# A planned Trainium2 kernel whose planner gets a transfer time for each kind of transfer

## The chip, the cores and the metric

The kernel runs on one core of a Trainium2 chip. The metric is the device time of one execution in microseconds (us); the time of a version is the median of several executions. TensorE (PE in the profile) multiplies matrices, VectorE (DVE), ScalarE (ACT) and GpSimd (POOL) work on elements, and SyncE (SP) issues most of the transfers (DMA) between memory and the core; GpSimd issues those that add into their target.

## The reference

The input `x` has 2048 rows of 512 numbers. The block normalises it and feeds it to two branches, whose product is added to `x`.

```python
x = A_x
xn = _layernorm(x, axis=-1)
s = _A_ref(xn, A_wqkv, A_wo)                   # linear attention, 32 heads of 16
g = _silu(_B_ref(xn, B_w1, B_w2, B_w3, B_w4))  # mixer with an MLP, 512 -> 1376 -> 512
return x + s * g

# A: phi = lambda t: where(t > 0, t + 1, exp(t)) + 1e-6, on q and k
kv = einsum("bhsd,bhse->bhde", pk, v);  z = einsum("bhsd->bhd", pk)
o = einsum("bhqd,bhde->bhqe", pq, kv) / (einsum("bhqd,bhd->bhq", pq, z)[..., None] + 1e-6)
s = o @ wo
# B: spatial shift of four groups of channels by +1, -1, +2, -2 rows, then the MLP
h = gelu(layernorm(x) @ w1);  x1 = x + shifted(h) @ w2
B = x1 + gelu(layernorm(x1) @ w3) @ w4
```

## The kernel before

Everything is float32. A product is made of three matmuls on parts rounded to a shorter type (`hi` and `lo`, written by `rounded` and `products`), and larger products use a seven-product scheme (`seven`). The 2048 rows are 16 tiles of 128 rows, in four blocks `b` of 512.

In the first part, to about 220 us, `x` and its transpose `xt` are loaded; keys and queries are formed and their Gram matrix is summed over all tiles in four accumulators (`gram`, tiles `g`); `w1` is centred (its column means are subtracted: `Weights.center` sums the four chunks of `w1` into `w1t` by gathers of GpSimd, the matmul `w1m` spreads the mean, and DVE subtracts it from the pieces `w_s`); `mix1` gives the tiles `h`, whose first matmuls need the centred pieces `w_0h`, `w_0l` and so on; `mix2` gives `x1`, which is normalised, turned by 32 x 32 blocks and written out (`Turned.put`). In the second part, for each block, `turn_y` fetches the turned tiles back in four pieces each (`y_0t`, `y_1t`), `up_pair` and `down` are the MLP, `turn_q` and `attend_pair` the attention (tiles `so`, accumulators `pbs` and others), and `gate` joins both and stores the result.

No engine's order is written by hand. The program first lists some 5,070 operations (`Plan.add`), each with its engine, the tiles that it reads and writes, and a duration; each is numbered in the order in which it is listed. `Plan.emit` then simulates the five engines and two queues and always emits the operation that can start first; among those that can start at about the same time it takes the one with the earliest due time. A matmul's due time is its place in the listed order; that of another operation is worked back from what needs it (`deadlines`, `backward`). The table `SOONER` then moves the due times of single operations by a quarter of a microsecond per unit (`nudged`). The emitted order is each engine's order on the chip; waits between engines are then semaphores.

What the simulation holds of a transfer is three lines in `emit`: one shared resource `dma`, on which transfers follow each other at 3.43 us per MB from SP and 4.59 from GpSimd, a fixed time to the landing, and a shortest time from issue to landing. An operation that needs a transfer is held back by up to `SAFE`, 2 us, behind the planned landing, if its due time leaves room for that. At most eight transfers of a queue are under way in the plan.

Of the kernel before, what the change touches and what calls it, by code (L numbers as in the profile page):

```python
# [11 lines left out]
ALU = mybir.AluOpType  # L12
AX = mybir.AxisListType

P = 128
# [11 lines left out]
class Tile:  # L27
# [16 lines left out]
    @property  # L44
    def all(self):
        return self[:, :]
# [5 lines left out]
class View:  # L52
# [3 lines left out]
    def get(self):  # L56
        return self.fn(self.tile.ap)
# [24 lines left out]

class Op:
    __slots__ = ("eng", "busy", "lat", "emit", "pre", "post", "tiles", "opens", "two", "table", "patience", "soon", "loads",
                 "nom", "due", "ready", "at", "end", "mb", "order")


class Plan:
# [9 lines left out]
    def add(self, eng, busy, lat, reads, writes, emit, two=False, table=None, mb=0.0):  # L98
        op = Op()
        op.eng, op.busy, op.lat, op.emit, op.two, op.table, op.mb = eng, busy, lat, emit, two, table, mb  # L100
        op.pre, op.post, op.tiles, op.opens = {}, [], {}, False
        op.order = len(self.ops)
        op.patience, op.soon = self.patience, False
        op.loads = any(isinstance(v, View) and v.tile.tag != "dram" for v in writes)
        for views, write in ((reads, False), (writes, True)):
            for v in views:
                if not isinstance(v, View):
                    continue
                t = v.tile
                op.tiles[t] = True  # L110
                op.opens |= not t.log and t.tag in self.counts
                for spans, other, wrote in t.log:
                    if other is op or not (write or wrote):
                        continue
                    if any(a < d and c < b for a, b in v.spans for c, d in spans):
                        flow = wrote and not (eng == "PE" and other.eng == "PE" and write)
                        op.pre[other] = op.pre.get(other, False) or flow
        for views, write in ((reads, False), (writes, True)):
            for v in views:
                if isinstance(v, View):  # L120
                    if write:
                        v.tile.log = [e for e in v.tile.log
                                      if not all(any(a <= c and d <= b for a, b in v.spans) for c, d in e[0])
                                      or e[1] is op]
                    v.tile.log.append((v.spans, op, write))
        for o in op.pre:
            o.post.append(op)
        for t in op.tiles:
            t.left += 1
        if eng == "PE":  # L130
            self.last_pe = op.order
        self.ops.append(op)
        return op
# [68 lines left out]
                 lambda: self.nc.vector.scalar_tensor_tensor(out.get(), a.get(), get(s), b.get(), op0=op0, op1=op1),  # L202
                 True, isinstance(s, View))

    def load(self, out, src, eng="SP"):
        mb = out.n * P * 4 / 1e6
        e = self.nc.scalar if eng == "ACT" else self.nc.sync
        self.add(eng, .42, 0, [], [out], lambda: e.dma_start(out.get(), src), mb=mb)

    def store(self, dst, src):  # L210
        mb = src.n * P * 4 / 1e6
        if isinstance(dst, View):
            return self.add("SP", .42, 0, [src], [dst], lambda: self.nc.sync.dma_start(dst.get(), src.get()), mb=mb)
        else:
            self.add("SP", .42, 0, [src], [], lambda: self.nc.sync.dma_start(dst, src.get()), mb=mb)

    def fetch(self, out, src):

        mb = out.n * P * 4 / 1e6
        self.add("SP", .42, 0, [src], [out], lambda: self.nc.sync.dma_start(out.get(), src.get()), mb=mb)  # L220

    def gather(self, out, src, share=1.0):

        mb = out.n * P * 4 / 1e6 * share
        return self.add("POOL", .8, 0, [src, out], [out],
                 lambda: self.nc.gpsimd.dma_start(out.get(), get(src), accum_op=ALU.add), mb=mb)  # L226

    GAP = .06  # L230
    PATIENCE = 2.5
# [38 lines left out]
    def emit(self, first, lead, reserve, window, ahead, table=()):  # L270
# [13 lines left out]
        port, dma = 0.0, 0.8  # L284
# [6 lines left out]
        while left:  # L291
# [5 lines left out]
            for e, cands in avail.items():  # L297
                picks = []
                low = INF
                for op in cands:  # L300
                    s = max(free[e], op.ready)
                    if op.mb:
                        s = max(s, under[e == "POOL"][0] + self.GAP)
                    if op.two and s < port:
                        s = port
                    if e == "POOL" and not op.mb and not op.two:
                        s = next((b + .02 for a, b in lock if a <= s < b), s)
                    if op.table is not None and op.table != table:
                        s = max(s, free[e] + 1.28)
                    ok = True  # L310
                    fresh = [t for t in op.tiles if t.ap is None]
                    for t in fresh:
# [7 lines left out]
                        s = max(s, q[need - 1][0] + self.GAP)  # L320
# [4 lines left out]
                        elif t.tag in lead:  # L325
# [3 lines left out]
                            s = max(s, op.due + slip - n - t.early)  # L329
# [12 lines left out]
                s, op = min(((s, op) for q, s, op in picks if q <= low + slack), key=lambda x: (x[1].due, x[1].order))  # L342
# [4 lines left out]
            s, op = best  # L347
            e = op.eng
# [12 lines left out]
            op.end = s + op.lat * k  # L361
            if op.mb:
                soft = e == "POOL"
                late = min(.92, 1.03 * max(0.0, dma - s))
                dma = max(dma, s + (.97 if soft else .06)) + op.mb * (4.59 if soft else 3.43)
                op.end = max(dma + (1.89 if soft else 1.29) + late, s + (4.08 if soft else 2.08 if op.loads else 2.2))
                under[soft].pop(0)
                under[soft].append(op.end)
            if op.two:
# [29 lines left out]
def linear_attn_gated_by_mixer(  # L399
# [22 lines left out]
    BT = QT * P  # L422
    FB = -(-F // P)
    W = 4
# [21 lines left out]
    pl = Plan(nc, pools, counts, ("acc", "mm"))  # L446

    def piece(name, dt=F32):
        return pl.new("p", name, dt, PIECE)[:, :512]
# [5 lines left out]
    def memory(name, width=512, rows=P):  # L455
        return pl.new("dram", name, F32, width, rows)
# [29 lines left out]
    def rounded(hi, lo, full, src=None):  # L486

        pl.act(hi, src or full, AF.Copy)
        split(lo, full, hi)
# [15 lines left out]
    arow, mrow = memory("arow", S + 2 * EDGE, 1), memory("mrow", S, 1)  # L505
# [136 lines left out]
    def join_a(b):  # L642

        t = ABC[b] = pl.new("ab", f"abc{b}", F32, BT + W)
        a = EDGE + b * BT - 2
        pl.fetch(t.all, arow[:, a:a + BT + W].via(lambda ap: ap.to_broadcast([P, BT + W])))

# [31 lines left out]
    def make_u(b):  # L679

        m = piece(f"um{b}")
        pl.fetch(m, mrow[:, b * BT:(b + 1) * BT].via(lambda ap: ap.to_broadcast([P, BT])))
        for c in range(NC):
            pl.tt(XT[b, c], XT[b, c], m, ALU.subtract)
            rounded(*(t[:, 2:2 + BT] for t in UT[b][c]), XT[b, c])
        q = {(t, k): [XT[b, 2 * k + c].cols(t * TH, (t + 1) * TH) for c in range(2)]
             for t in range(2) for k in range(2)}
        U[b] = {n: [both([v[:, 2:2 + BT] for v in UT[b][2 * k + c]], t * TH, (t + 1) * TH) for c in range(2)]
                for n, t, k in (("a11", 0, 0), ("a12", 0, 1), ("a22", 1, 1))}
        s = [piece(f"us{b}_{k}") for k in range(4)]  # L690
        parts = [[v.cols(c * TH, (c + 1) * TH) for c in range(2)] for v in s]
        for n, u, v, op in ((0, q[1, 0], q[1, 1], ALU.add), (1, parts[0], q[0, 0], ALU.subtract),
                            (2, q[0, 0], q[1, 0], ALU.subtract), (3, q[0, 1], parts[1], ALU.subtract)):
            for c in range(2):
                pl.tt(parts[n][c], u[c], v[c], op, eng=SUMS)
            hl = rounds(f"us{b}_{n}")
            rounded(*hl, s[n])
            U[b][f"s{n + 1}"] = [both(hl, c * TH, (c + 1) * TH) for c in range(2)]
# [42 lines left out]
    class Turned:  # L741
# [15 lines left out]
        def take(self):  # L757
            self.w = w = 512 * self.n
            t = self.t = pl.new("w" if self.n == 2 else "p", f"{self.name}t", F32, 1024 if self.n == 2 else PIECE)
            nb = P // RB  # L760
            for n in range(nb):
                src = self.d.cut([(0, 512)], w // nb, lambda ap, n=n: ap.rearrange(
                    "(a k) (b f) -> b k a f", k=RB, b=nb)[n])
                dst = t.cut([(n * w // nb, (n + 1) * w // nb)], w // nb, lambda ap, n=n: ap[
                    n * RB:(n + 1) * RB, :w].rearrange("k (a f) -> k a f", f=P))
                pl.fetch(dst, src)

        def part(self, c0, c1):

# [627 lines left out]
    b = NQ - 1  # L1397
# [6 lines left out]
    for base, s in ((0, 1), (DH - 1, -1)):  # L1404
        v = bmask.all.via(lambda ap: ap.rearrange("p (h d) -> p h d", d=DH))
        pool(.5, [v], v, lambda v=v, base=base, s=s: g.affine_select(
            out=v.get(), in_=v.get(), compare_op=ALU.is_ge, fill=0.0, base=base,
# [33 lines left out]
    for b in range(NQ):  # L1441
# [46 lines left out]
        else:  # L1488
# [3 lines left out]
            t = piece(f"xi{i}", F32R)  # L1492
# [13 lines left out]
                gate(b * QT + QT - 1, a, o, D // 2, late=True, by_dma=False, whole=o > 0)  # L1506

    SOONER = (
# [3 lines left out]
    )  # L1512
    pl.emit(first=6.0, lead={"p": 14.0, "w": 14.0, "ab": 10.0}, reserve={"p": 20, "w": 1, "ab": 0}, window=12.0,
            ahead=6.0, table=SOONER)
# [37 lines left out]
```

## Time and profile before

| | us |
|---|---|
| median of three executions | 514.07 |
| the three executions | 514.64, 514.07, 512.39 |
| the profiled execution | 512.43 |
| its span, from the first to the last instruction | 510.7 |
| TensorE busy in the span | 502.9 |
| VectorE, ScalarE, GpSimd busy | 426.3, 348.9, 91.2 |

The granted TensorE clock was 1.00 in the whole span. A row of a list of waits names the engine and the tile that waited, after the arrow what it waited for, and then the total time, the number of times and the longest one. A row of the chain of waits gives start, duration and what the time was spent on. "L" and a number is a line of the kernel; most operations are recorded by a few helpers, so one goes by the names of the tiles.

### The profile page before, as it was taken

The numbers are of one execution on the slowest core, as the hardware profiler recorded it, in microseconds if no ns is written. First come the engines' busy times: TensorE is split into PE (matmuls) and PEld (weight loads), VectorE is DVE, ScalarE is ACT, GpSimd is POOL, SyncE is SP. The second block draws the span as 40 slices with busy tenths as digits, with TensorE's granted clock in tenths as the row PEclk, the third lists the DMA queues.
The fourth block names the chain that finished last, engine by engine and source line by source line (L and its number), as shares of the span: only waits on it lengthen the run. The fifth ranks groups of instructions, "written<-read, shape, count | busy, mean of one in ns | idle before, by whom it ended". The sixth has DMA issues, their size and how long they took to land.

```text
span 510.7 us, 8948 instructions
## 1 busy us (share of the span) xinstructions
PE 502.9 (98%) x2972; PEld 437.9 (86%) x2972; DVE 426.3 (83%) x885; ACT 348.9 (68%) x703; POOL 91.2 (18%) x145
## 2 busy tenths in 40 slices
PE   9998999999999999999999999999999999999995
PEld 7777777898888788889989898999898998999985
DVE  6999999999699986999999978956779656898645
ACT  5899699676697785866876668655488453765621
POOL 1258411663134122021000020000020000200000
PEclk9999999999999999999999999999999999999999
DMA  8889947189994799799767758475495595758604
GB/s 270 310 185 226 303 151 167 41 201 295 278 284 92 239 292 270 199 271 313 247 204 205 224 137 280 160 215 154 164 230 183 181 222 166 182 185 265 195 14 111
DMA packets 76619, 106.17 MB, mean 208 GB/s; under 512 B 8224, under 2 KB 31292, under 8 KB 76572
## 3 DMA queue, kind: packets, MB, share of 16 engines
q1 hardware_dynamic: 68940, 91.70, 56.4%
q0 software_dynamic: 7632, 13.90, 16.1%
q8 instruction: 23, 0.38, 0.3%
q14 instruction: 24, 0.20, 0.1%
HBM read 67.41 MB, written 29.77 MB: 190 GB/s over the span
## 4 chain that ended last, share of the span: by engine, by line
PE 86%; DVE 5%; ACT 5%; DMA 2%; issue 1%; SPq 1%; DVEq 0%; ACTq 0%
PE acc L148 23%; PE pb L148 11%; PE h L148 8%; PE g L148 7%; PE pbk L148 6%; PE pe L148 5%; PE pbm L148 4%; PE pbs L148 4%; PE pek L148 3%; PE pa L148 3%; PE pem L148 2%; PE a L148 2%; PE pes L148 2%; DMA y_1t<-y_1d 2%; PE pak L148 1%
## 5 line engine op out<-in xcount | busy, mean ns | idle before, releaser
L226 POOL DMA_DIRECT2D th<-in_x x14 | 12.2, 939 | 248.0 <-DVE so L192 64.8
L170 ACT ACTIVATE th<-xo 128x512 f32<-128x512 f32 (+1 forms) x16 | 9.8, 620 | 26.8 <-DVE xo L192 26.6
L192 DVE TENSOR_TENSOR xo<-acc,xo 128x512 f32<-128x512 f32 (+1 forms) x16 | 10.5, 671 | 16.9 <-PE acc L148 16.8
L170 ACT ACT_TABLE_LOAD x18 | 23.1, 1283 | 1.1 <-PEq L1543 0.8
L170 ACT ACTIVATE gf<-gf 128x512 f32<-128x512 f32 (+1 forms) x40 | 20.6, 525 | 0.8
L226 POOL DMA_DIRECT2D o<-x x16 | 14.0, 873 | 40.1 <-DVE o L192 15.5
L226 POOL DMA_DIRECT2D zacc<-kr x16 | 13.9, 867 | 40.6 <-DMA zacc<-kr 22.2
L170 ACT ACTIVATE p<-pb 128x256 f32<-128x256 f32 x20 | 7.6, 382 | 14.2 <-PE pb L148 14.0
L604 POOL TENSOR_TENSOR rs<-w,nhalf 128x4 f32<-128x4 f32 (+2 forms) x10 | 10.1, 1012 | 35.5 <-DVE w L197 32.6
L170 ACT ACTIVATE p<-pe 128x256 f32<-128x256 f32 x20 | 7.7, 385 | 11.9 <-PE pe L148 11.9
L170 ACT ACTIVATE ht<-ht 128x512 f32<-128x512 f32 x16 | 9.7, 623 | 8.9 <-DVE ht L192 8.9
L192 DVE TENSOR_TENSOR gf<-pa,p 128x256 f32<-128x256 f32 x20 | 8.4, 420 | 7.8 <-PE pa L148 7.5
L170 ACT ACTIVATE x<-x,nm,rs 128x512 f32<-128x512 f32 x16 | 12.9, 807 | 2.5 <-DVE nm L202 2.5
L598 DVE BATCH_NORM_STATS2 st<-o 128x6 f32<-128x512 f32 x16 | 10.9, 686 | 3.5 <-DMA o<-x 3.4
L192 DVE TENSOR_TENSOR gf<-u,pe 128x256 f32<-128x256 f32 x20 | 8.2, 410 | 6.5 <-PE pe L148 6.5
L202 DVE SCALAR_TENSOR_TENSOR kr<-kt,kr 128x512 f32<-128x512 f32 x16 | 10.9, 688 | 1.8 <-ACT kt L170 1.7
L170 ACT ACTIVATE y<-o,nm,rs 128x512 f32<-128x512 f32 x16 | 11.9, 807 | 0.5 <-DVE nm L202 0.5
L192 DVE TENSOR_TENSOR ht<-h,abc 128x512 f32<-128x512 f32 x16 | 10.9, 683 | 0.8 <-PE h L148 0.6
L202 DVE SCALAR_TENSOR_TENSOR pq<-pq,qr 128x512 f32<-128x512 f32 x12 | 8.1, 683 | 4.1 <-ACT pq L170 4.0
L170 ACT ACTIVATE u<-pb 128x256 f32<-128x256 f32 x20 | 7.7, 383 | 5.5 <-PE pb L148 5.5
L202 DVE SCALAR_TENSOR_TENSOR th<-th,so 128x512 f32<-128x512 f32 (+1 forms) x17 | 10.9, 653 | 0.5
L202 DVE SCALAR_TENSOR_TENSOR pq<-pq,rd 128x512 f32<-128x512 f32 x16 | 10.9, 688 | 0.2
(1679 smaller groups left out, 2235.5 us busy)
## 6 DMA issues: line engine op xcount, KB each, us to landing
w_s<-in_w SPq DMA_DIRECT2D x28, 256.0 KB, 4.3
x<-in_x SPq DMA_DIRECT2D x16, 256.0 KB, 5.3
zacc<-kr POOLq DMA_DIRECT2D x16, 256.0 KB, 5.9
o<-x POOLq DMA_DIRECT2D x16, 256.0 KB, 4.9
x1d<-o SPq DMA_DIRECT2D x16, 256.0 KB, 4.2
xo<-x1d SPq DMA_DIRECT2D x16, 256.0 KB, 5.0
xt<-in_xt SPq DMA_DIRECT2D x15, 256.0 KB, 5.0
out<-th SPq DMA_DIRECT2D x15, 256.0 KB, 3.4
```

The costliest lines, as they stand in the source:

```text
L148: lambda: nc.tensor.matmul(out.get(), lhs.get(), rhs.get(), start=start, stop=stop, skip_group_check=more))
L170: nc.scalar.activation(out.get(), src.get(), func, scale=get(scale), **kw)
L192: self.vec(eng, out, [a, b], lambda: self.e(eng).tensor_tensor(out.get(), a.get(), b.get(), op=op), True)
L202: lambda: self.nc.vector.scalar_tensor_tensor(out.get(), a.get(), get(s), b.get(), op0=op0, op1=op1),
L226: lambda: self.nc.gpsimd.dma_start(out.get(), get(src), accum_op=ALU.add), mb=mb)
L598: pl.add("DVE", .62, .69, [xv], [st], lambda: nc.vector.bn_stats(st.get(), xv.get()))
L604: lambda: g.tensor_tensor(out.get(), src.get(), nh.get(), op=ALU.pow))
```

## The change

The list of operations stays the same. Each transfer gets a kind, with its own time per MB: load (from an input), fetch (from a scratch tensor), row (one row spread over all partitions), turn (the pieces of a turned tile), store and gather. The constants around it change too, in a new method `landing`; the planned issue time of GpSimd's transfers goes from 0.8 to 0.6 us; and the table `SOONER` is another one.

```diff
-    def load(self, out, src, eng="SP"):
-        mb = out.n * P * 4 / 1e6
-        e = self.nc.scalar if eng == "ACT" else self.nc.sync
-        self.add(eng, .42, 0, [], [out], lambda: e.dma_start(out.get(), src), mb=mb)
+    def move(self, eng, out, src, kind, mb, reads, writes, emit):
+        op = self.add(eng, .42 if eng == "SP" else .6, 0, reads, writes, emit, mb=mb)
+        op.rate = self.RATE[kind]
+        return op
+
+    def load(self, out, src):
+        return self.move("SP", out, src, "load", out.n * P * 4 / 1e6, [], [out],
+                         lambda: self.nc.sync.dma_start(out.get(), src))
...
     def gather(self, out, src, share=1.0):
-
-        mb = out.n * P * 4 / 1e6 * share
-        return self.add("POOL", .8, 0, [src, out], [out],
-                 lambda: self.nc.gpsimd.dma_start(out.get(), get(src), accum_op=ALU.add), mb=mb)
-
-
+        return self.move("POOL", out, src, "gather", out.n * P * 4 / 1e6 * share, [src, out], [out],
+                         lambda: self.nc.gpsimd.dma_start(out.get(), get(src), accum_op=ALU.add))
+
+    RATE = {"load": 2.92, "fetch": 3.5, "row": 4.18, "turn": 5.7, "store": 2.44, "gather": 5.79}
+
+    def landing(self, op, s, dma):
+
+        soft = op.eng == "POOL"
+        dma = max(dma, s + (.33 if soft else 0)) + op.mb * op.rate
+        late = min(1.11, .68 * max(0.0, dma - s))
+        return dma, max(dma + (1.36 if soft else 1.25) + late, s + (3.77 if soft else 1.97 if op.loads else 1.68))
...
                 soft = e == "POOL"
-                late = min(.92, 1.03 * max(0.0, dma - s))
-                dma = max(dma, s + (.97 if soft else .06)) + op.mb * (4.59 if soft else 3.43)
-                op.end = max(dma + (1.89 if soft else 1.29) + late, s + (4.08 if soft else 2.08 if op.loads else 2.2))
+                dma, op.end = self.landing(op, s, dma)
...
     SOONER = (
-        23, 127, 94, 16, 119, -16, 128, 16, 132, 2, 183, 4, 291, 8, 322, 16, 333, 72, 394, -4, 412, -32, 418, -64,
-        423, -101, 424, -64, 426, -17, 427, 44, 429, 8, 483, 16, 612, 16, 749, 32, 1599, -8, 2185, 32, 2781, -8,
-        3582, 16, 3853, 32, 4261, 8, 4798, -32, 4917, 8, 4980, -8, 4994, -32, 4996, 8,
+        9, 64, 23, 17, 94, 32, 119, -8, 128, 16, 132, 2, 183, 4, 269, -8, 291, 8, 333, 72, 336, 16, 357, 2,
+        394, -4, 415, -124, 448, 8, 455, 32, 612, 16, 1599, -8, 1728, -8, 1976, 4, 2287, 64, 2350, 4, 2393, 16,
+        2431, 32, 3017, 32, 3582, 16, 3853, 32, 3932, -8, 4086, 8, 4662, 16, 4798, -32, 4917, 8,
     )
```

The calls in `join_a` and `make_u` pass the kind "row", and those in `Turned.take` the kind "turn". Some of the numbered operations: 9 is the store of a zero edge of `arow`, 23 the first load of `xt`, 412, 415 and 418 are matmuls of the Gram matrix of tile 3, 423 and 424 split `w1t` into `w1mh` and `w1ml`, 426 is the matmul `w1m` on the second, 427 and 429 subtract it from pieces of `w1`, and 455 is the copy `kq_0h`.

More of the change, by code (lines that the diff above doesn't have):

```diff
@@ L84 @@
     __slots__ = ("eng", "busy", "lat", "emit", "pre", "post", "tiles", "opens", "two", "table", "patience", "soon", "loads",
-                 "nom", "due", "ready", "at", "end", "mb", "order")
+                 "nom", "due", "ready", "at", "end", "mb", "order", "rate")
 class Plan:
@@ L102, in add @@
         op.order = len(self.ops)
-        op.patience, op.soon = self.patience, False
+        op.patience, op.soon, op.rate = self.patience, False, 0.0
         op.loads = any(isinstance(v, View) and v.tile.tag != "dram" for v in writes)
@@ L203, in stt @@
                  True, isinstance(s, View))
-    def load(self, out, src, eng="SP"):
-        mb = out.n * P * 4 / 1e6
-        e = self.nc.scalar if eng == "ACT" else self.nc.sync
-        self.add(eng, .42, 0, [], [out], lambda: e.dma_start(out.get(), src), mb=mb)
-    def store(self, dst, src):
[L211 to L215, printed above, removed]
@@ L217, in fetch @@
-    def fetch(self, out, src):
-        mb = out.n * P * 4 / 1e6
-        self.add("SP", .42, 0, [src], [out], lambda: self.nc.sync.dma_start(out.get(), src.get()), mb=mb)
-    def gather(self, out, src, share=1.0):
-        mb = out.n * P * 4 / 1e6 * share
-        return self.add("POOL", .8, 0, [src, out], [out],
-                 lambda: self.nc.gpsimd.dma_start(out.get(), get(src), accum_op=ALU.add), mb=mb)
+    def move(self, eng, out, src, kind, mb, reads, writes, emit):
+        op = self.add(eng, .42 if eng == "SP" else .6, 0, reads, writes, emit, mb=mb)
+        op.rate = self.RATE[kind]
+        return op
@@ new lines, in load, with fetch @@
+    def load(self, out, src):
+        return self.move("SP", out, src, "load", out.n * P * 4 / 1e6, [], [out],
+                         lambda: self.nc.sync.dma_start(out.get(), src))
+    def store(self, dst, src):
+        return self.move("SP", dst, src, "store", src.n * P * 4 / 1e6, [src], [dst] if isinstance(dst, View) else [],
+                         lambda: self.nc.sync.dma_start(get(dst), src.get()))
+    def fetch(self, out, src, kind="fetch"):
+        return self.move("SP", out, src, kind, out.n * P * 4 / 1e6, [src], [out],
+                         lambda: self.nc.sync.dma_start(out.get(), src.get()))
@@ L645, in join_a @@
         a = EDGE + b * BT - 2
-        pl.fetch(t.all, arow[:, a:a + BT + W].via(lambda ap: ap.to_broadcast([P, BT + W])))
+        pl.fetch(t.all, arow[:, a:a + BT + W].via(lambda ap: ap.to_broadcast([P, BT + W])), "row")
     UT = {}
@@ L681, in make_u @@
         m = piece(f"um{b}")
-        pl.fetch(m, mrow[:, b * BT:(b + 1) * BT].via(lambda ap: ap.to_broadcast([P, BT])))
+        pl.fetch(m, mrow[:, b * BT:(b + 1) * BT].via(lambda ap: ap.to_broadcast([P, BT])), "row")
         for c in range(NC):
@@ L765, in take @@
                     n * RB:(n + 1) * RB, :w].rearrange("k (a f) -> k a f", f=P))
-                pl.fetch(dst, src)
+                pl.fetch(dst, src, "turn")
         def part(self, c0, c1):
```

## The prediction

> **What bounds the kernel now.** I read the page first, then a table of windows, then TensorE's own waits, and then the chain of waits around each of them.
>
> ```profile
> span 510.7 us, 8948 instructions
> PE 502.9 (98%) x2972; PEld 437.9 (86%) x2972; DVE 426.3 (83%) x885; ACT 348.9 (68%) x703; POOL 91.2 (18%) x145
> PE 86%; DVE 5%; ACT 5%; DMA 2%; issue 1%; SPq 1%; DVEq 0%; ACTq 0%
> ```
>
> TensorE is busy for 502.9 of 510.7 us, and the chain that ended last runs on it for 86% of the span. The change leaves the 2972 matmuls as they are, so an order can only win back what lies between them: 510.7 - 502.9 = 7.8 us. The table of windows says where that is (first column: the stretch; then its length and the busy time of each engine, PE first).
>
> ```profile
> core 0: us, PE busy (x) PEld busy (x) DVE busy (x) ACT busy (x) POOL busy (x), PEclk, DMA share, GB/s
> 0.00:14.00 14.00, 12.96 (x50) 9.98 (x51) 9.42 (x17) 8.15 (x15) 2.24 (x14) 1.00 0.83 282
> 14.00:42.80 28.80, 27.51 (x120) 21.25 (x118) 27.44 (x69) 27.01 (x57) 14.55 (x24) 1.00 0.82 222
> 42.80:64.00 21.20, 21.13 (x89) 16.46 (x90) 21.09 (x39) 16.00 (x28) 13.14 (x26) 1.00 1.01 294
> 64.00:220.00 156.00, 156.00 (x832) 132.33 (x831) 141.59 (x309) 120.35 (x226) 45.99 (x65) 1.00 0.76 209
> 220.00:420.00 200.00, 200.00 (x1321) 180.47 (x1320) 164.52 (x334) 132.54 (x283) 10.09 (x11) 1.00 0.73 212
> 420.00:426.00 6.00, 5.69 (x42) 5.02 (x42) 4.80 (x10) 3.54 (x10) 0.00 (x0) 1.00 0.63 145
> 426.00:505.60 79.60, 79.60 (x530) 72.38 (x528) 56.16 (x110) 40.93 (x89) 5.22 (x6) 1.00 0.57 164
> 505.60:510.70 5.10, 0.00 (x1) 0.00 (x0) 1.30 (x4) 0.38 (x1) 0.00 (x0) 0.96 0.35 126
> ```
>
> Of the 7.8 us, 1.04 lie ahead of the first matmul, 1.29 just ahead of 42.8 us, 0.07 in the next 21 us, 0.31 between 420 and 426 us, and 5.10 behind the last matmul. From 64 to 420 us and from 426 us to the end TensorE has no idle time at all. The ends of matmuls are modelled, so a little may be hidden in a busy stretch, but not much. TensorE's list of waits names the inner two:
>
> ```profile
> PE h L148 <- ACT w_0h L170: 1.3, 1, 1.3
> PE warm L148 <- POOL ones L511: 1.0, 1, 1.0
> PE pbs L148 <- ACT u2s L170: 0.3, 1, 0.3
> ```
>
> The 1.0 us ahead of the warm-up matmuls waits for a memset and belongs to no transfer. The last 5.10 us are the last gate and its store, one operation behind another. So what can be had in the profiled execution is 1.29 + 0.07 + 0.31 = 1.7 us.
>
> **The wait at 42.8 us.** It ends on an ACT copy, `w_0h`, the first piece of the centred `w1`. The timeline of ACT and DVE, and GpSimd's at 31 us, show what stood ahead of it (start, duration, engine, line, operation):
>
> ```profile
> 36.34 1.32 ACT L170 ACTIVATE qe<-qt,ns 128x512 f32<-128x512 f32 x2
> 37.56 1.14 ACT L170 ACTIVATE qe<-qe 128x512 f32<-128x512 f32 x2
> 38.60 0.61 ACT L170 ACTIVATE w1mh<-w1t 128x512 fp32r<-128x512 f32 x1
> 39.13 1.32 ACT L170 ACTIVATE qr<-qt,rs 128x512 f32<-128x512 f32 x2
> 40.35 0.71 ACT L170 ACTIVATE qe<-qt,ns 128x512 f32<-128x512 f32 x1
> 40.97 0.61 ACT L170 ACTIVATE u_1h<-xt 128x512 fp32r<-128x512 f32 x1
> 42.01 0.61 ACT L170 ACTIVATE w_0h<-w_s 128x512 fp32r<-128x512 f32 x1
> ...
> 41.14 1.88 DVE L202 SCALAR_TENSOR_TENSOR w_s<-w1m,w_s 128x512 f32<-128x512 f32 x3
> ...
> 30.95 0.90 POOL L226 DMA_DIRECT2D w1t<-in_w  x1
> 31.55 0.95 POOL L707 CAST u_0h<-hal 128x2 fp32r<-128x2 f32 x1
> ```
>
> `w1mh` needs the sum `w1t`, whose last gather is issued at 30.95 us; the list of DMA issues below gives these gathers a median of 5.1 us to landing, so the sum is there at about 36.1 us. ACT takes it up at 38.60 us, 2.5 us later, behind four copies of queries (`qe`, 36.34 to 38.70). The stall is thus a matter of order on ACT and DVE, not of a late transfer: in 14 to 42.8 us ACT is busy for 27.01 and DVE for 27.44 of 28.80 us. Putting `w1mh` ahead of the `qe` pairs would bring the chain forward by up to 2.5 us, and the matmul that waits needs 1.29.
>
> **The wait at 423 us.** The chain of waits shows a transfer behind this one:
>
> ```profile
> 414.64 7.74 DMA y_1t<-y_1d
> ...
> 422.48 0.63 ACT yb123h L170
> 423.11 0.28 ACT u2s L170
> ...
> 423.44 0.97 PE pbs L148 x6
> ```
>
> `yb123h` sits at the head of ACT's in-order queue until the fourth piece of `y_1t` has landed, 7.74 us after its issue, and `u2s`, which releases the accumulator `pbs`, stands behind it. The old model gave each such 128 KB piece 0.131 x 3.43 = 0.45 us, the new one 0.131 x 5.7 = 0.75, so four of them together land 1.2 us later in the new plan; a planner that believes this puts `u2s` ahead of `yb123h`, or the fetch earlier.
>
> **The change, part by part.** *The rates.* No instruction comes or goes, so nothing in it has a cost on the chip; what changes is what the planner believes, and with it each engine's order. One 256 KB transfer is 0.262 MB: on SP it was 0.90 us, and becomes 0.77 (load), 0.92 (fetch), 1.10 (row) or 0.64 (store); a gather goes from 1.20 to 1.52. Medians to landing at 256 KB (`y_1t` 128 KB) are these:
>
> ```profile
> x<-in_x SPq DMA_DIRECT2D x16, 256.0 KB, 5.3
> o<-x POOLq DMA_DIRECT2D x16, 256.0 KB, 4.9
> xo<-x1d SPq DMA_DIRECT2D x16, 256.0 KB, 5.0
> out<-th SPq DMA_DIRECT2D x15, 256.0 KB, 3.4
> xs<-in_x SPq DMA_DIRECT2D x8, 256.0 KB, 7.7
> y_1t<-y_1d SPq DMA_DIRECT2D x16, 128.0 KB, 5.4
> w1t<-in_w POOLq DMA_DIRECT2D x3, 256.0 KB, 5.1
> ```
>
> They bear out the kinds at the ends: a store lands in 3.4 us, and `y_1t` takes 5.4 for half the bytes. They don't show a gather (`o`, 4.9 us) as dearer than a fetch (`xo`, 5.0), and they do not bear out a cheap load: `x` needs 5.3 us and `xs` 7.7, but both hold the time in the queue. I take the direction as right and the size of the load as doubtful.
>
> [...]
>
> *GpSimd's issue*, 0.8 to 0.6 us in the plan: the rows at 30.95 and 31.55 start 0.60 us apart, so it comes nearer to the chip. Nothing on the chain waits for it; cost 0, at most one issue's 0.2 us either way.
>
> *The hand-set due times* (SOONER; numbers are operations in program order, a unit is 0.25 us). Those on `w1`'s centring go (423, 424, 426, 427, 429), and with them two of the Gram matmuls put off (412, 418); another Gram matmul (415, the third chunk of tile 3) is put off by 31 us, which leaves TensorE other work for just the place where it waits 1.29 us; `kq_0h` (455) gets due 8 us earlier and joins ACT's queue there. The first load of `xt` (23) is hurried by 4.25 us in place of 31.75, and a store of the zero edge of `arow` (9) by 16 us. This store goes to SP's queue among the first loads and costs one issue, 0.4 us at most for what is queued behind. Bounds for the opening, then: between all of the 1.29 us won, and a wait that is longer than now by one transfer. The longest row of the same kind, `xs` at 7.7, is 2.4 us over `x` at 5.3; so -1.3 to +2.4. I take -1.3, nearest to the rows above, for these show 2.5 us of ACT work that could stand behind.
>
> *The turn's rate*, at 423 us: -0.3 us, bounds -0.3 and +0.7; the upper one is where ACT's queue blocks for as long as the chain rows from 422.48 to 423.44 show, 0.96 us, in place of 0.31.
>
> *The executions.* The profiled one took 512.43 us, 1.73 more than its span of 510.7; the three timed ones took 514.64, 514.07 and 512.39. The median is 1.64 us above the profiled time. Two executions sit at 512.4 and two at 514 or above, with the same program, so some wait comes and goes; the place where the profile shows a transfer eating its whole margin is the turn before 423 us, and there are others like it after each block of 512 rows. A plan that prices turns, fetches and gathers higher leaves more room there. I put 1.2 of the 1.64 us down as won; bounds 0 and 1.64. This is the weakest term.
>
> The sum: in the profiled execution 512.43 - 1.3 - 0.3 = 510.8; against the median 514.07 - 1.3 - 0.3 - 1.2 = 511.3 us, 0.54% faster. About 0.5%, or 2.57 us, is what a measurement of this kernel can tell from no change.
>
> **The rivals.** *No room (same).* The two inner waits go, or are exchanged for others as small, but the coming and going of 1.64 us has nothing to do with the plan: 514.07 - 1.6 = 512.5 us. It covers too the case that the new table gives much the same order: outside 3 us of waits TensorE is seamless, and 356 us of the middle have nothing to win. For it: the windows. Against it: the spread of the executions at an unchanged program.
>
> *Late landings in the opening (slower).* Between 14 and 64 us ACT and DVE have next to no idle time (DVE 21.09 of 21.20 us in the second stretch), and each engine keeps its order. The new plan holds loads to be 15% cheaper than the old one (2.92 against 3.43), so it may put an operation at the head of ACT or DVE whose load isn't there yet, and all that is queued behind (the `w1` pieces, `u` pieces, keys) is late by as much; nothing later makes it up, since TensorE has no idle time to give. One such landing costs 7.7 - 5.3 = 2.4 us if it falls on a chain that TensorE waits for. Two of them, one ahead of `w_0h` with the 1.29 us still there, and one in the 20 us behind it, give 514.07 + 4.8 = 518.9 us; one gives 516.5. It decides from where loads land over 2 us later than planned, for the planner keeps 2 us (SAFE) behind every transfer when the due time allows. For it: load rows that differ by 2.4 us at one size. Against it: the rows of PE's waits hold no transfer at all now, so the margins hold.
>
> **How the numbers follow.** The forecast gets 0.45, no room 0.30, late landings 0.25. Faster by over 0.5% needs under 511.5 us, which only the forecast gives; its own range runs from 510.8, with all three terms full, less about 1.2 that seamless stretches may hide (an estimate: the six `pbs` matmuls at 423.44 take 0.97 us, and a few such stretches would have to shrink), to 511.5. Late landings pass 516.6 with a little over one. The range, 509.6 to 518.0, leaves out about 0.05 below and 0.12 above, the dearer half of late landings. Chances: faster 0.45, same 0.30, slower 0.25.
>
> **What would show it.** Right: TensorE's waits without `w_0h`, or with under 0.5 us there; ACT taking `w1mh` up within about 1 us of the landing of `w1t`; no wait near 423 us; TensorE's busy time again near 502.9 us and a span near 509; executions closer together. Wrong: a wait at `h` of over 1.3 us, a new wait on a DMA in the first 64 us, or a seamless stretch of the middle that has gaps. If the span falls by 1.6 us and the median doesn't move as far, the term for the executions is what failed.

## The result, and the profile after

| | before | changed |
|---|---|---|
| median of 22 executions, us | 512.41 | 514.36 |
| lowest to highest | 511.33 to 514.98 | 512.70 to 516.52 |
| profiled execution, span | 512.43, 510.7 | 513.31, 511.6 |

The changed kernel is slower: the ratio of its time to that before is 1.0028, 95% interval 1.0015 to 1.0040. (The ratio of the two means, 514.44 and 513.01, is the same; that of the medians is 1.0038.) The change is smaller than the 0.5% that the prediction named, but clear of no change, and it goes the other way. The median before is also 1.66 us below that of the three executions on which the prediction stood; with 22 executions it lies where the profiled one lay.

The page of the changed kernel, its span, two of its engines and the chain:

```profile
span 511.6 us, 8924 instructions
PE 503.6 (98%) x2972; PEld 438.5 (86%) x2972; DVE 425.3 (83%) x885; ACT 348.2 (68%) x703; POOL 93.8 (18%) x145
PE 95%; DMA 2%; DVE 2%; ACT 0%; issue 0%; SPq 0%
```

```profile
0.00:14.00 14.00, 12.53 (x47) 9.49 (x47) 8.69 (x16) 8.28 (x14) 2.23 (x14) 1.00 0.84 273
14.00:42.80 28.80, 28.16 (x120) 21.53 (x119) 26.07 (x67) 25.96 (x53) 15.21 (x27) 1.00 0.82 213
42.80:64.00 21.20, 19.99 (x87) 15.77 (x86) 21.19 (x39) 16.47 (x30) 10.06 (x24) 1.00 1.05 299
64.00:220.00 156.00, 156.00 (x822) 131.88 (x821) 141.17 (x308) 120.44 (x226) 50.13 (x64) 1.00 0.77 208
220.00:420.00 200.00, 200.00 (x1322) 180.76 (x1321) 164.43 (x335) 130.72 (x280) 10.97 (x12) 1.00 0.74 213
420.00:426.00 6.00, 6.00 (x48) 5.68 (x46) 4.32 (x10) 5.32 (x13) 0.00 (x0) 1.00 0.76 189
426.00:506.00 80.00, 80.00 (x531) 72.64 (x531) 57.32 (x111) 40.63 (x89) 5.16 (x6) 1.00 0.57 162
```

In the windows (columns as before) the middle is as seamless as it was, the 0.31 us at 423 us are gone, and all that TensorE idles between its first and its last matmul lies in the first 64 us. There DVE is busy for 26.07 us between 14 and 42.8 us, where it was busy for 27.44. TensorE's waits:

```profile
PE h L148 <- ACT w_0h L170: 1.2, 1, 1.2
PE warm L148 <- POOL ones L514: 1.0, 1, 1.0
PE g L148 <- DVE k3l L202: 0.5, 1, 0.5
PE k L148 <- DMA wk_s<-in_wqkv: 0.4, 1, 0.4
```

The wait for `w_0h` is still there, and two are new: one ahead of the Gram matmuls of tile 3 (on the keys `k3l`), and one ahead of the first matmul `k` (on the first weights `wk_s`). Followed back from `h`, the chain of waits of the changed kernel between 29 and 45 us reads in extract (start, duration, what):

```profile
29.63 3.46 DMA mrow<-cr
...
33.11 4.04 DMA um<-mrow
...
37.17 0.69 DVE xt L192
37.86 0.60 DVE kr L202
...
40.27 0.60 DVE k3l L202
...
42.13 0.60 DVE w1ml L192
42.73 0.61 DVE xt L192
43.33 0.69 DVE w_s L202
...
44.05 0.64 ACT w_0h L170
...
44.73 1.42 PE h L148 x5
```

Two transfers in a row, a store of one row of means (`mrow`) and its fetch onto all partitions (`um`), now hold DVE in this execution, and all that is queued on DVE behind the first subtraction of `um`: the keys of tile 3, `w1ml`, the centring `w_s`. DVE's timeline has the wait in its brackets, and the kernel before has the same subtraction behind the other work, with no wait:

```profile
37.17 0.69 DVE L192 TENSOR_TENSOR xt<-xt,um 128x512 f32<-128x512 f32 x1 [1.34 <-DMA um<-mrow]
37.77 0.69 DVE L202 SCALAR_TENSOR_TENSOR kr<-kt,kr 128x512 f32<-128x512 f32 x1
```

```profile
36.59 0.69 DVE L202 SCALAR_TENSOR_TENSOR k3l<-kr,k3h 128x512 fp32r<-128x512 f32 x1
...
39.00 0.68 DVE L192 TENSOR_TENSOR xt<-xt,um 128x512 f32<-128x512 f32 x1
```

The kernel's own planner says why. These are its planned times beside the traced ones (the planner's clock is taken to start 0.68 us after that of the traces):

```
                      um: planned issue, landing    planned    traced     DVE's first subtraction of um
before                34.96, 40.10                  5.14 us    4.02 us    planned at 40.65
changed               32.69, 35.78                  3.09 us    4.04 us    planned at 35.85
end of TensorE's work, planned: before 504.03, changed 502.74; on the chip, less 0.68: 504.92 and 506.25
```

The old model overrated this transfer by 1.1 us, the new one underrates it by 0.95. By plan the changed order was 1.3 us better; on the chip it is 1.3 us worse. The same turn shows at the first `h`: planned at 44.37 before and 43.44 in the changed kernel, it came at 42.09 and 44.05 on the planner's clock.

### The profile page after: what moved, and what is told of

Its sections match the earlier page's. It is cut to its first block, busy times and chain, and to the rows that moved or that the text cites. A ratio compares the mean times of both kernels' runs of the same rounds, so it can differ in the third digit from the quotient of the medians.

```text
span 511.6 us, 8924 instructions
## 1 busy us (share of the span) xinstructions
PE 503.6 (98%) x2972; PEld 438.5 (86%) x2972; DVE 425.3 (83%) x885; ACT 348.2 (68%) x703; POOL 93.8 (18%) x145
## 4 chain that ended last, share of the span: by engine, by line
PE 95%; DMA 2%; DVE 2%; ACT 0%; issue 0%; SPq 0%
PE acc L148 23%; PE pb L148 11%; PE h L148 9%; PE g L148 7%; PE pbk L148 7%; PE pe L148 6%; PE pbs L148 5%; PE pbm L148 5%; PE pek L148 3%; PE pa L148 3%; PE k L148 2%; PE pem L148 2%; PE pes L148 2%; PE a L148 2%; PE pak L148 2%; PE q L148 2%
## 5 line engine op out<-in xcount | busy, mean ns | idle before, releaser
L607 POOL TENSOR_TENSOR au<-pu,nhalf 128x4 f32<-128x4 f32 x4 | 8.2, 2058 | 19.9 <-DVE pu L197 14.6
L170 ACT ACTIVATE so<-pbs 128x256 f32<-128x256 f32 x8 | 3.1, 385 | 12.7 <-PE pbs L148 12.7
L192 DVE TENSOR_TENSOR so<-pas,p1s 128x256 f32<-128x256 f32 x8 | 3.4, 420 | 9.7 <-PE pas L148 4.7
```

The costliest lines, as they stand in the source:

```text
L170: nc.scalar.activation(out.get(), src.get(), func, scale=get(scale), **kw)
L192: self.vec(eng, out, [a, b], lambda: self.e(eng).tensor_tensor(out.get(), a.get(), b.get(), op=op), True)
L607: lambda: g.tensor_tensor(out.get(), src.get(), nh.get(), op=ALU.pow))
```

## The experiments

The theory (A): the loss is made in the opening, because the changed plan counts on landings that come later; and it is the cheap price of the load that does it, not the table (A1). A narrower form (E): it is the one wait on `um`. Rivals: the long second part (B), the table (A2), the fixed times (C), the ratio of the kinds (D), and for the last runs something else that the price of the row moves (F).

**Which part of the program.** Two kernels have both models and change from one to the other at 64 us of planned time; the table's entries to operation 749 go with the first model.

```diff
-                dma, op.end = self.landing(op, s, dma)
+                new = s >= 64.0
+                dma, op.end = (self.landing if new else self.before_landing)(op, s, dma)
+                if soft and not new:
+                    free[e] = s + .8
```

`before_opening` has this text, `after_opening` has `s < 64.0`. On every engine their planned orders are those of the kernels that they are named for up to 95 us at least.

> The order of the kernel before up to 64 us, planned on from there with the changed rates and the later part of the changed table. Theory A (the loss is made in the opening, where the changed plan counts on transfers landing sooner than they do): like before, 512.4 us or less, within 0.1% of it. Theory B (the loss is made in the long second part, by collisions of transfers that come and go): like after, about 514 us, 0.25% over before.

> The order of the changed kernel up to 64 us, planned on from there with the rates before and the later part of the table before. Theory A: like after, about 514 us, 0.25% over before, with the DVE wait on um of about 1.3 us at 36 us. Theory B: like before, 512.4 us, within 0.1%.

Measured: `before_opening` 1.0001 (0.9986 to 1.0015), though with a median of 513.25 us, 0.7 over that of before. So the changed rates and table cost at most 0.15% from 64 us on, and B falls. `after_opening` came out at 1.0067 (1.0042 to 1.0091) in six executions, slower than either theory had it. Its windows show 1.06 us that TensorE idles between 64 and 420 us, where both parents are seamless; the rest of its loss is open.

```profile
64.00:220.00 156.00, 155.65 (x821) 131.08 (x820) 140.47 (x307) 120.03 (x225) 50.88 (x65) 1.00 0.76 207
220.00:420.00 200.00, 199.29 (x1310) 178.95 (x1310) 161.31 (x327) 127.78 (x276) 10.71 (x12) 1.00 0.71 207
```

Theory A expected a wait of DVE on `um` of 1.3 us here, and its profiled execution has none. The order is that of the changed kernel, but SP could issue the fetch 2.50 us after the store of `mrow`, in place of 3.48, and DVE took up the first subtraction of `um` without a wait:

```profile
29.39 0.27 SPq L216 DMA_DIRECT2D mrow<-cr  x1
31.89 0.34 SPq L220 DMA_DIRECT2D um<-mrow  x1
...
35.51 0.69 DVE L192 TENSOR_TENSOR xt<-xt,um 128x512 f32<-128x512 f32 x1
```

From the first `k` to the first `h` it needed 37.77 us, 1.72 less than the changed kernel's profiled execution. So the wait costs about that much in this pair, and the order alone doesn't bring it about: it takes a late landing too. How many of the changed kernel's executions have it, one profile can't tell.

**Rates or table.** `new_rates_old_table` is the changed kernel with the old `SOONER`, `old_rates_new_table` the kernel before with the new one; nothing else is edited.

> The changed rates with the table of due times before. Theory A1 (the rates themselves are too hopeful in the opening): about 514 us, 0.25% over before, PE's end over 2.5 us behind the plan's 503.96. Theory A2 (only the changed table puts the um subtraction too early): within 0.1% of before. A table that was set for other rates may add up to 1 us under both.

> The rates before with the changed table. Theory A1: near before, 512.4 to 513.2 us, PE's end about 1 us behind the plan's 503.98. Theory A2: about 514 us, with a wait of DVE on um.

Measured: 1.0025 (1.0010 to 1.0041) and 1.0001 (0.9985 to 1.0017). The rates (with the fixed times and GpSimd's issue) carry the loss; the table carries none.

**Which rate.** From the kernel before, with a rate for each kind, all at the old values but those named; table, fixed times and GpSimd's issue stay the old ones:

```diff
-                dma = max(dma, s + (.97 if soft else .06)) + op.mb * (4.59 if soft else 3.43)
+                dma = max(dma, s + (.97 if soft else .06)) + op.mb * op.rate
```

`only_load` has load 2.92 and else 3.43 and 4.59; `all_but_load` has load 3.43 and else the changed rates. `before_less_08` is the kernel before with every landing 0.8 us sooner:

```diff
-                op.end = max(dma + (1.89 if soft else 1.29) + late, s + (4.08 if soft else 2.08 if op.loads else 2.2))
+                op.end = -.8 + max(dma + (1.89 if soft else 1.29) + late, s + (4.08 if soft else 2.08 if op.loads else 2.2))
```

> The kernel before, with one number changed: loads at 2.92 us per MB in the plan in place of 3.43; table, other rates and fixed times as before. The order changes in the opening, and the second half of TensorE's order is that of before. Theory A1 (the cheaper load is what spends the margin in the opening): 513.7 to 514.3 us, 0.2 to 0.3% over before, with transfers in the opening landing on average within 1 us of the plan in place of 2.6 us ahead. Rival C (the fixed times and the cheap store do it, the load rate does not): within 0.1% of before, 512.5 us.

> The kernel before with all the changed rates but that of the load, which stays at 3.43; fixed times and table as before. DVE's order is that of before up to 42 us. Theory A1: within 0.1% of before, about 512.5 us. Rival C: 0.2% over or more.

> The kernel before, with every transfer planned to land 0.8 us sooner; rates, their ratios and the table stay. Theory A1 (what counts is the margin, whatever the kind): slower, 513.5 to 514.5 us, 0.2 to 0.4%. Rival D (what counts is how the kinds stand to each other, or a table that fits its rates): within 0.1% of before, 512.5 us.

Measured: 1.0039 (1.0020 to 1.0057), 1.0003 (0.9982 to 1.0024) and 1.0040 (1.0020 to 1.0060). With the old table the load's rate alone makes a loss of this size, all the other rates together make none, and 0.8 us off every landing with all ratios kept make it too; D falls, and C falls in so far as it held the load's rate to be harmless (the fixed times were not changed alone). Matching the planned transfers with the traced ones in order, those planned before 64 us landed on average 2.60 us ahead of the plan before (48 landings of 69 can be traced), 0.98 us ahead in `only_load` and 0.69 us ahead in `before_less_08`; in the changed kernel they landed 0.25 us behind it (33 of 70). From issue to landing alone, the old model was 0.82 us too long in the opening and the changed one 0.05 too long. `after_opening`, with the same plan up to 64 us, landed 0.61 us ahead of it, and there the changed model was 0.42 too long: the changed prices are nearer on average, by an amount that differs from one execution to the next, and the plan that used the wrong ones is the better.

**The one wait.** `changed_row_plus_15` is the changed kernel with 1.5 us more to the landing of a row, which moves little but DVE's first subtraction of `um`: in the planned orders 24 of DVE's 885 operations stand at another place, 14 of ACT's 677, 17 of GpSimd's 141, 7 of TensorE's 2940 and none of SP's, most of them between 35 and 64 us. `changed_row_again` is the same program, measured another time.

```diff
-        return dma, max(dma + (1.36 if soft else 1.25) + late, s + (3.77 if soft else 1.97 if op.loads else 1.68))
+        return dma, (1.5 if op.rate == self.RATE["row"] else 0) + max(dma + (1.36 if soft else 1.25) + late, s + (3.77 if soft else 1.97 if op.loads else 1.68))
```

> The changed kernel, with 1.5 us more to the planned landing of a row (um) alone. SP's order and TensorE's second part stay as they are; on DVE the first subtraction of um moves behind three other operations at 36 to 38 us, and DVE no longer waits for um. Theory E (that one wait is what the changed kernel loses): 513.1 us, 1.2 us under the changed kernel, within 0.15% of before. Theory A1 in general (the margin is gone at many places): 513.8 to 514.3 us, still about 0.2% over before or more.

> The changed kernel with 1.5 us more to the planned landing of a row, once more on another call. If it is the better version: 511.7 to 512.2 us, 0.1 to 0.35% under before. If the first result was chance: within 0.1% of before.

Measured: 0.9977 (0.9961 to 0.9994) and 0.9990 (0.9970 to 1.0009), medians 511.95 and 511.89 us. The loss is gone, and more: 2.4 us of median where theory E had counted on 1.2. This is the best of the versions, ahead of the changed kernel both times, and of the one before in one interval of two. Its DVE takes `um` up behind three others without a wait (no bracket on the row), and `h` starts at 43.24 us in place of 44.73:

```profile
35.43 0.69 DVE L202 SCALAR_TENSOR_TENSOR kr<-kt,kr 128x512 f32<-128x512 f32 x1
36.04 1.29 DVE L192 TENSOR_TENSOR kq<-wq_s,kq 128x512 f32<-128x512 f32 x2
37.24 0.68 DVE L192 TENSOR_TENSOR xt<-xt,um 128x512 f32<-128x512 f32 x1
```

The mirror, `before_um_less_40`, puts the wait into the kernel before:

```diff
+                if any(t.name[:2] == "um" for t in op.tiles):
+                    op.end -= 4.0
```

> The mirror: the kernel before, with the planned landing of um alone 4 us sooner. The plan's end moves by 0.1 us only; on DVE the first subtraction of um moves ahead of k1l and of the keys of tile 3. Theory E (an um operation at the head of DVE's queue before um is there costs the changed kernel its time): DVE waits about 1 us on um near 35 us, TensorE starts h about 44.5 us in place of 43, and the time is 513.5 to 514.3 us, 0.2 to 0.35% over before. Rival F (it isn't this wait; the row's price changed something else): within 0.1% of before, 512.6 us.

Measured: 1.0026 (1.0011 to 1.0040), and the wait as expected, from the lists of waits of DVE and TensorE (two more waits of TensorE come with it):

```profile
DVE xt L192 <- DMA um<-mrow: 1.2, 1, 1.2
PE h L148 <- ACT w_0h L170: 1.6, 1, 1.6
PE g L148 <- DVE k1l L202: 1.0, 1, 1.0
PE h L148 <- POOL u_3l L710: 0.7, 1, 0.7
```

So theory E is borne out from both sides: give the changed kernel that landing and it recovers, take it from the kernel before and it loses what the change lost. The first is the cleaner edit. The mirror takes off 4.0 us in place of 1.5, and moves 187 of TensorE's operations, most of them behind 100 us.

**Is it that wait everywhere?** `new_rates_old_table_row_plus_15` puts the same 1.5 us into the changed rates with the old table; `changed_plus_08` is the changed kernel with 0.8 us on every landing (`return dma, .8 + max(...)`).

> The changed rates with the table before, and 1.5 us more to the planned landing of a row. Theory E: 512.6 to 513.0 us, within 0.1% of before, where without the 1.5 us it was 0.25% over; no wait of DVE on um. Rival F: still 514 us.

> The changed kernel with 0.8 us more to the planned landing of every transfer. Its plan ends 2.8 us later than the changed one (505.57 in place of 502.74). Theory A1 in general (margin everywhere is what helps): 512.5 us or less, at most that of before. Theory E (one wait): the wait on um goes, but the order is a worse one by the plan, so 513 to 514.5 us, no better than 0.1% over before.

Measured: 1.0030 (1.0010 to 1.0049), a miss for E, and 1.0045 (1.0028 to 1.0063), which goes against A1 in its general form. With the old table the wait on `um` is gone and the loss is not: there TensorE waits twice in three microseconds, ahead of `w1m` and of `h`, and its granted clock falls to 0.50. The timeline and the windows of `only_load` (the number behind POOL's is the granted clock), which has the same two waits, show it best:

```profile
40.99 0.40 PE L148 MATMUL g<-k3h,x3l 128*128 128x512 f32 x1
42.54 0.50 PE L148 MATMUL w1m<-w1ml,onesr 128*128 128x512 f32 x1 [1.15 <-DVE w1ml L192]
44.48 0.49 PE L148 MATMUL h<-u_0h,w_0h 128*128 128x512 f32 x1 [1.45 <-ACT w_0h L170]
...
46.49 0.63 PE L148 MATMUL h<-u_1h,w_1h 128*128 128x512 f32 x1
46.92 0.63 PE L148 MATMUL h<-u_1l,w_1h 128*128 128x512 f32 x1
```

```profile
45.30:46.00 0.70, 0.70 (x3) 0.58 (x2) 0.70 (x2) 0.70 (x2) 0.70 (x2) 0.54 1.14 184
46.00:48.00 2.00, 2.00 (x6) 1.54 (x5) 2.00 (x5) 2.00 (x5) 0.80 (x2) 0.50 1.05 261
48.00:49.00 1.00, 1.00 (x4) 0.77 (x4) 1.00 (x2) 1.00 (x3) 0.00 (x0) 0.62 1.10 315
```

The times of the single executions show how much of the miss is the clock. Seven of the twelve of `new_rates_old_table_row_plus_15` have a mean granted clock of 0.996 and took 514.62 to 516.69 us; the five at 0.999 or 1.000 took 512.79 to 513.39, on average 513.11, near the mean of the kernel before, 512.89. Without the row's 1.5 us, in `new_rates_old_table`, the four at 0.996 or less took 515.41 to 515.99 and the eight others 513.39 to 514.13. This split was made after the fact, but no execution of the kernel before or of the changed one has a clock below 0.997: the changed kernel's loss is not one of the clock, and that of the three kernels with the cheap load and the old table is so in part. Their agreement with it in size says less than it seems to.

And 0.8 us on every landing take the wait on `um` away at the price of a plan that ends 2.8 us later. What it loses shows in part: `h` starts at 43.96 us, 1.19 later than before, and TensorE idles 0.40 us between 470 and 490 us, where it idled nowhere.

All in one table: the ratio to the time before, the time in the profiled execution from the first matmul `k` to the first `h` (both from TensorE's timeline), and DVE's wait on `um`.

| kernel | ratio | k to h, us | wait on um, us |
|---|---|---|---|
| before | 1 | 38.15 | 0 |
| before_opening | 1.0001 | 38.70 | 0 |
| old_rates_new_table | 1.0001 | 38.10 | 0 |
| all_but_load | 1.0003 | 37.83 | 0 |
| changed_row_plus_15, again | 0.9977, 0.9990 | 37.77, 38.55 | 0 |
| changed | 1.0028 | 39.48 | 1.3 |
| only_load | 1.0039 | 39.29 | 0.7 |
| before_less_08 | 1.0040 | 39.94 | 1.3 |
| before_um_less_40 | 1.0026 | 40.46 | 1.2 |
| new_rates_old_table | 1.0025 | 39.10 | 0.6 |
| the same, row plus 1.5 | 1.0030 | 39.59 | 0 |
| changed_plus_08 | 1.0045 | 38.64 | 0 |
| after_opening | 1.0067 | 37.77 | 0 |

But for the last two, which lose elsewhere, the kernels that are no slower need 38.7 us or less for this stretch and the slower ones 39.1 or more. Each row is one execution, and the same program lies 0.8 us apart in its two (37.77 and 38.55), so the border between 38.7 and 39.1 is a hint and no more; what carries the argument is the one clean edit, `changed_row_plus_15`, with its repetition.

## Why the prediction was wrong

*What bounds the kernel* was right: only what TensorE idles can be won or lost, and the middle stays seamless in both.

*The opening, -1.3 us*, is the step that failed. It read the wait at 42.8 us rightly as one of order on ACT and DVE, and then took the changed table to set that order well, because 2.5 us of other work stood ahead of `w1mh`. (It was 3.6: the last gather of `w1t` landed at 34.98 us, 4.03 us after its issue, and not after the median of 5.1.) The changed kernel took `w1mh` up at 40.59 us, 4.70 us behind the landing there (35.89), so later than before and not sooner. The wait stayed at 1.21 us, and `h` came 1.97 us later (44.73 for 42.77), of which 0.63 us is a later first matmul (5.25 for 4.62) that the order of the transfers doesn't explain: both kernels issue the same first nine. The prediction asked which work could stand behind; it didn't ask at which landing the new plan would put the head of a queue. Its rival of late landings had the mechanism, an operation at the head of DVE whose transfer isn't there, with all behind it late. It had the condition, 2 us late, wrong: the subtraction of `um` was planned 0.07 us behind its planned landing, since its hurried due time leaves the `SAFE` 2 us no room. A landing 0.68 us behind the plan and a DVE 0.7 us ahead of it were enough for the wait of 1.34 us. And it looked for it among the loads; the transfer that came late is a row, whose own rate had gone up, from 3.43 to 4.18. It was the cheap load before it on the one shared planned queue that brought its landing forward: with the load's price alone changed, `um` is planned to land 2.25 us after its issue in place of 5.14; with all prices changed but the load's, 5.40.

*The doubt on the load's price* pointed the right way for a wrong reason. The cheap load is not false on average (the 26 loads traced in the opening before took 1.01 us less than the plan gave them, the 16 in the changed kernel still 0.32 less); it spent a margin that a false price had given.

*The turn at 423 us, -0.3 us*, came out as forecast, 6.00 of 6.00 us busy, and ACT now takes `u2s` ahead of `yb123h`, as the prediction had it:

```profile
424.06 0.40 ACT L170 ACTIVATE u2s<-pbs 128x256 f32<-128x256 f32 x1
424.32 0.65 ACT L170 ACTIVATE yb123h<-y_1t 128x512 fp32r<-128x512 f32 x1
```

That the turn's rate won this is not shown. `old_rates_new_table` has the same order of the two at the old rate, and `only_load`, `before_less_08` and `before_um_less_40` keep `yb123h` ahead and don't wait either: their pieces of `y_1t` landed 4.0 to 4.5 us after the issue, not 7.1 to 7.4. The 0.31 us was in good part a matter of the one execution that was profiled.

*The executions, -1.2 us*, had no ground. The profiled execution, at 512.43, was the usual one: the median of 22 is 512.41. Three executions can't carry a term of 1.2 us where single ones lie 3.7 us apart. What makes some of them slower by about 2 us, in the kernel before too, no run here tells; there it isn't the clock, for executions of 512.2 and of 514.4 us both have it at 0.999.

*The sum.* From the first `k` to the first `h` the opening lost 1.33 us where the prediction had 1.3 won; 512.4 + 1.3 - 0.3 = 513.4, where it had 511.3. The later first matmul would make it 514.1, near the median of 514.36, but that matmul is later by chance as far as is known, and the profiled execution itself took 513.31. Between the changed kernel (514.36) and the one with the row put right (511.9) lie 2.4 us, of which the stretch from `k` to `h` shows 0.9 to 1.7; the rest is left open.

## What to carry to other kernels

An estimate that is right on average leaves many transfers late (20 of the 33 traced in the changed kernel's opening, 2 of 48 before), and an engine that takes its work in order passes a late one on to all that stands behind (DVE's wait of 1.34 us on one row came with 1.33 us more from the first `k` to the first `h`); a planner's price should lie at the late end of the landings for a transfer that is taken up at the head of a full engine's queue. Put the margin where a late landing hurts: 1.5 us on one row won 0.4 to 0.5% of the changed kernel's time, and 0.8 us on every transfer won nothing. When a cost model is made truer and the result slower, compare planned and traced landings one by one, and look at shared queues: the price that changed need not be that of the transfer that comes late. And profile more than one execution: a wait that a landing decides can be in one and not in the next.

## What the runs showed of the hardware

In the three kernels with the cheap load and the old table the granted clock fell to 0.50 for about 3.4 us (in `only_load`, worked out from the clock of its windows, from 45.36 to 48.76 us), and in `only_load` matmuls of 512 columns started 0.43 us apart there in place of 0.23. TensorE's waits ahead of `w1m` and `h`, with a single matmul between them, were 1.15 and 1.45 us in `only_load`, 0.7 and 1.7 in `new_rates_old_table`, and 0.3 and 1.7 in the one with the row's 1.5 us. Waits of 1.2 to 1.6 us ahead of `h` in the other eleven profiles left the clock at 1.00 in all their windows up to 64 us. What decides between a fall and none, and why some executions of a program have it and others don't, is not shown.

The first matmul on the first weights started at 4.62 us before and at 5.25 in the changed kernel, there after a wait of 0.42 us on `wk_s`, though the first nine issues of the two are the same; in `old_rates_new_table` it started at 5.70, after a wait of 1.02.

A store of one row of 512 means, 2 KB, held the fetch that reads it back for 2.64 us before (29.58 to 32.22), 3.48 us in the changed kernel (29.63 to 33.11) and 2.50 us in `after_opening` (29.39 to 31.89); the fetch then took 4.02 us more to land before, and 4.04 in the changed kernel.
